# Windowed attention and routed experts: router columns copied on ScalarE, 64-row transposes, another order of stores and constants

## Chip, cores and metric

The kernel runs on one core of a Trainium2 chip. The metric is the device time of one execution in microseconds (us). The kernel before has three timed runs: 412.46, 412.88 and 413.97 us, median 412.88.

## What is computed

Attention over q, k, v of shape (8, 8, 576, 64) with a causal window of 64 positions, then a skip test, a router of 8 experts with one expert per token, and that expert's two-layer network:

```python
scores = (q @ k.transpose(0, 1, 3, 2)) / sqrt(64)
mask = (rel >= 0) & (rel < 64)               # rel = query position - key position
attn = softmax(where(mask, scores, -1e9))
x = (attn @ v).transpose(0, 2, 1, 3).reshape(4608, 512)
out = x.copy()
xc = x[x @ w_skip > 0]
probs = softmax(xc @ w_gate)                 # 8 experts
e_idx = argmax(xc @ w_gate)
y = probs[e_idx] * (relu(xc @ w1[e_idx]) @ w2[e_idx])
out[x @ w_skip > 0] = xc + y
```

## The kernel before

The 4608 tokens are cut into 36 tiles of 128 tokens, each of two blocks of 64 positions. Eight tiles of nine hold neighbouring blocks of one batch. The ninth (tiles 8, 17, 26 and 35) holds the last block of two batches.

The order of the work is written out by hand in a loop over `t` (lines 1182 to 1222), the "iterations" below. Every engine works through its own instructions in the order in which they are written there, and so do the queues from which transfers are issued (SP for nearly all loads and stores, POOL for the gathers and scatters). Iteration `t` writes, in this order:

- the loads that are due (`load_qk`, `load_v`, and their "tail" forms for the ninth tiles), issued from SP;
- `score(t + 1)` (lines 231 to 260): PE adds the mask band and writes q k^T for 8 heads into the two banks of `ps`, of which there are two copies; four quarters of PE's array, 64 by 64, work side by side;
- the gate products (`gate`, `gate_t`, lines 327 to 355): they work out v times the router's weights, 8 columns for experts and one for the skip test, which become columns 65 to 73 of each head in `vm`; column 64 is ones. Their results share the PSUM tag "t", two banks, with the transposes below;
- `lessen(t)` (lines 262 to 269): DVE takes the row maximum `mx` and subtracts it into `s`;
- `raise_e(t)` (line 273): ACT takes the exponential;
- `tile_out(t - 2)` with `av_tile` (lines 375 to 413): PE multiplies the transposed probabilities `ptm` with `vm` into `av`, of which there is one copy, two halves of 64 columns side by side; DVE then reads the sums of the probabilities in column 64 and forms `r`, their reciprocal (L395, L396), multiplies the 512 attention columns by it into `x` (L397), and the 72 router columns by it into `lh` (L403); `x` has four buffers;
- `transpose_p(t - 1)` (lines 275 to 283): PE transposes the probabilities of 8 heads, four at a time into one bank, and ACT copies each bank to `ptm`;
- `lower` and `tail_lower`: ACT copies that move the key block shared by two tiles.

Finished `x` tiles are stored to `out` by `store()` (lines 417 to 425), two tiles late (`SDELAY`), from SP. A tile of two batches is stored by one transfer (L425).

Routing works on groups of 8, 8, 6, 6 and 8 tiles. `lh` of a group holds 9 columns for 8 heads; `route` (line 505) adds up the heads, on GpSimd for the first four groups (`pool_part`, line 467) and on DVE for the last (`vector_part`, line 427). It then picks the expert and counts places; some of its steps are spread over several iterations by `yield`. After group 3 (tile 21) GpSimd works out `perm`, the order of the first two experts, for which SP waits before the first expert weights (L837). `load_constants` puts tables into `cf` and `vals` in iteration 3; `set_constants` makes small tables of them on GpSimd in iteration 5. `xgs` are nine buffers of 128x512, cleared in iteration 1; they later take gathered rows and, in between, pieces of the routing.

In the last two tiles, outside the loop, `transpose_p` writes into both banks of a `ps` tile (`into`). Then the expert stage runs to the end: weights are loaded in pieces of 512 KB (`raw`), split into a high and a low part, and multiplied with gathered rows.

Of the kernel before, what the change touches and what calls it, by code (L numbers as in the profile page):

```python
# [8 lines left out]
F32 = mybir.dt.float32  # L9
# [4 lines left out]
ALU = mybir.AluOpType  # L14
# [4 lines left out]
B, H, S, HD = 8, 8, 576, 64  # L19
N, D, E, F = 4608, 512, 8, 1024  # L20
P = 128
NB = S // 64
NT = N // P
# [19 lines left out]
NPOOL = 28  # L43
# [7 lines left out]
AHEADQ, AHEADV = 5, 4  # L51
SDELAY = 2
# [91 lines left out]
def window_attention_moe(ctx: ExitStack, tc, a, out):  # L144
    nc = tc.nc
# [6 lines left out]
    psum = ctx.enter_context(tc.tile_pool(name="psum", bufs=1, space=PSUM))  # L152
# [10 lines left out]
    ident = gid[:, 1]  # L163
# [22 lines left out]
    xp = rt.enter_context(tc.tile_pool(name="xp", bufs=2, side="right"))  # L186
    sm = rt.enter_context(tc.tile_pool(name="sm", bufs=3, side="right"))
# [83 lines left out]
    def raise_e(t):  # L271
        s = ss[t]
        nc.scalar.activation(s, s, AF.Exp, scale=0.125)  # L273

    def transpose_p(t, into=None):
        s = ss.pop(t)
        ptm = ptp.tile([P, 8, P], F32, name="ptm")
        for r in range(2):
            pt = into[:, r] if into is not None else psum.tile([P, 4, P], F32, name="pt", tag="t", bufs=2)
            for p in range(4):  # L280
                nc.tensor.transpose(pt[:, p], s[:, 4 * r + p], ident)  # L281
            nc.scalar.copy(ptm[:, 4 * r : 4 * r + 4], pt)  # L282
        pts[t] = ptm

    ss, pts, vs = {}, {}, {}
# [86 lines left out]
    def tail_lower(m, z):  # L372
        nc.scalar.copy(vms["t", m][0][:64, z], vms[4 * m + 2 * z + 1][64:, 3])

    def av_tile(t, lh, sums, av=None):
        blks = tiles[t]
        ptm, win = pts.pop(t), vs.pop(t)
        x = xp.tile([P, D], F32, name="x", bufs=XPB)
        if av is None:
            av = pav.tile([P, 2, 512], F32, name="av")  # L380
        banks["av"] = av
        for h in range(8):
            for hf in range(2):
                nc.tensor.matmul(  # L384
                    av[64 * hf : 64 * hf + 64, h // 4, (h % 4) * VW : (h % 4 + 1) * VW],
                    ptm[:, (h % 2) * 4 + h // 2, 64 * hf : 64 * hf + 64],
                    win[hf][:, h],
                    start=True,
                    stop=True,
                )  # L390
        if sums:
            sums()
        r = sm.tile([P, 2, 4], F32, name="r")
        src = av[:, :, : 4 * VW].rearrange("p z (h c) -> p z h c", c=VW)
        nc.vector.tensor_scalar(r, src[..., 64], 1e-9, None, op0=ALU.add)  # L395
        nc.vector.reciprocal(r, r)  # L396
        pace[0] = nc.vector.tensor_tensor(  # L397
            x.rearrange("p (z h c) -> p z h c", z=2, c=64),
            src[..., 0:64],
            r.unsqueeze(3).to_broadcast([P, 2, 4, 64]),  # L400
            op=ALU.mult,
        )
        nc.vector.tensor_tensor(  # L403
            lh.rearrange("p c (z h) -> p z h c", z=2),
            src[..., 65:74],
            r.unsqueeze(3).to_broadcast([P, 2, 4, 9]),
            op=ALU.mult,
        )
        if sums:
            sums()  # L410
        stores.append((x, blks))
        while len(stores) > (SDELAY if t < NT - 6 else 0):
            store()

    stores = []

    def store():
        x, ((b0, i0), (b1, i1)) = stores.pop(0)
        r0 = b0 * S + i0 * 64
        r1 = b1 * S + i1 * 64  # L420
        if r1 == r0 + 64:
            nc.sync.dma_start(out[r0 : r0 + P], x)
        else:
            both = out.rearrange("(b s) d -> b s d", s=S)[b0 : b1 + 1, i0 * 64 : i0 * 64 + 64]
            nc.sync.dma_start(both, x)  # L425

    def vector_part(t0, n, lh):
        lg = sm.tile([P, n, 9], F32, name="lg")
# [73 lines left out]
        yield "sums"  # L502
        return nd, ohb, gs

    def route(t0, n, lh):
        bn = lambda z: z.unsqueeze(1).to_broadcast([P, n, E])
        first_part = pool_part if t0 < NPOOL else vector_part
        nd, ohb, gs = yield from first_part(t0, n, lh)
        if t0 + n < NT:
            pr = banks["av"][:, 1, PRAT : PRAT + (n + 1) * E].rearrange("p (n e) -> p n e", e=E)  # L510
        else:
            pr = banks["late"].tile([P, n + 1, E], F32, name="pr", tag="g", bufs=1, padded_shape=[P, 64, E])
        nc.tensor.matmul(pr[:, 0:n], trib, ohb, start=True, stop=False, skip_group_check=True)
        for j in range(n):
            m = n - j
            nc.tensor.matmul(
                pr[:, j + 1 :],
                onesb,
                ohb[:, j : j + 1].to_broadcast([P, m, E]),
                start=False,  # L520
                stop=(j == n - 1),
                skip_group_check=True,
            )
        yield "added"
        ds = sm.tile([P, n, E], F32, name="gds")
        nc.vector.tensor_tensor(ds, pr[:, 0:n], bn(base), op=ALU.add)
        nc.vector.tensor_tensor(base, base, pr[:, n], op=ALU.add)
        nc.vector.reciprocal(ent[:, t0 : t0 + n, 1], gs)
        assert t0 < NCLOSE or "closed" in tables
        if t0 + n == NT:  # L530
            tables["counted"] = True
        here = rows[:, t0 : t0 + n]
        nc.gpsimd.tensor_tensor(ds, ds, ohb, op=ALU.mult)
        add_up(here, ds, E)
        nc.gpsimd.tensor_tensor(here, here, nd, op=ALU.add)
        later.append(enter(t0, n))
# [209 lines left out]
    xgs = [early.tile([P, D], F32, name=f"xg{i}") for i in range(NXG)]  # L746
# [8 lines left out]
    late = []  # L755
# [21 lines left out]
    def sums():  # L777
        step(late, held)
# [1 line left out]
    def listing():  # L780
        step(later, held2)

    grp = [0, 0, None]
    heads = [sum(GRP[:i]) for i in range(len(GRP))]

    def tile_out(t, av=None):
        if t in heads:
            n = GRP[heads.index(t)]
            grp[:] = [t, n, xp.tile([P, n, 9, H], F32, name="lh")]
        t0, n, lh = grp  # L790
        behind = None
        if held[0] == "sums" and held[1] >= WAIT.get(t0, 2):
            behind = sums
        elif held2[0] == "lists" and held2[1] >= LWAIT:
            behind = listing
        av_tile(t, lh[:, t - t0], behind, av)
        progress[0] = t + 1
        if t + 1 == t0 + n:
            late.append(route(t0, n, lh))

    progress = [0]

# [336 lines left out]
    first_of = [9 * (n // 4) + 2 * (n % 4) for n in range(NG)]  # L1139
    with tc.manual_schedule():  # L1140
# [16 lines left out]
        def when_at(t, f, n):  # L1157
            at.setdefault(max(t, 0), []).append((f, n))

        gate_at, lower_at, after_at = {}, {}, {}  # L1160
        for n in range(NG):
            if n >= 2:
                if n > 2:
                    when_at(first_of[n] - AHEADQ, load_qk, n)
                when_at(first_of[n] - AHEADV, load_v, n)
            gt = first_of[n] + 1 if n < 2 else first_of[n] - (2 if n > NSLOW else n == NSLOW)
            gate_at.setdefault(gt, []).append((gate_v, n))
            (after_at if n == 1 else gate_at).setdefault(gt + (n != 1), []).append((gate_vt, n))
            lower_at.setdefault(gt + 1, []).append((lower, n, 1))
            if n % 2:  # L1170
                lower_at.setdefault(gt + (1 if n == 3 else 2 * (n > 3)), []).append((lower, n, 0))
        for m in range(B // 2):
            z = 2 * (m == 0)
# [8 lines left out]
        for t in range(NT - 1):  # L1182
            m, r = divmod(t, 9)
            for f, n in at.get(t, ()):
                f(n)
            score(t + 1)
            gates = gate_at.get(t, ())
            if t == 0:
                keep_busy(5)
            for f, n in gates:  # L1190
                f(n)
            if t in (1, 2):
                transpose_p(t - 1)
            routes(1)
            if t != 3:
                lessen(t)
            raise_e(t)
            if t == 2:
                lessen(3)
            if BOTH <= t < NT - 2:  # L1200
                drip()
            if t >= 2:
                tile_out(t - 2)
            for f, n in after_at.get(t, ()):
                f(n)
            drip()
            routes(1)
            if t > 2:
                transpose_p(t - 1)
            if t == 1:  # L1210
                clear_rows()
            if t == 3:
                load_constants()
            if t == 5:
                set_constants()
            routes(1)
            for f, n, j in lower_at.get(t, ()):
                f(n, j)
            for _ in range(U0.count(t)):
                weight_dma_first()  # L1220
            if t == NT - 3:
                weight_hi(0)
# [197 lines left out]
    with tc.If(more > 0):  # L1420
        with tc.For_i(0, more, 1) as i:
# [15 lines left out]
            for qi in range(NQ):  # L1437
                both = []
                for w in range(2):
                    n = 2 * qi + w  # L1440
# [56 lines left out]
```

## Time and profile before

| | us |
|---|---|
| median of three runs | 412.88 |
| profiled execution | 411.98 |
| its span, first to last instruction | 410.2 |
| PE busy | 390.3 |
| DVE busy | 303.2 |
| ACT busy | 218.8 |
| GpSimd (POOL) busy | 154.2 |

Engines: PE is the matmul engine and PEld its weight loads, DVE the vector engine, ACT the scalar engine, POOL is GpSimd, SP issues transfers. "L397" is line 397 of the kernel. "x<-av,r" names what an instruction writes and reads. A busy engine is not necessarily a bottleneck: matmuls are pipelined, so that PE counts as busy over most of the span. The chain of work that ended last follows, from the last instruction back, what each step waited for. A share of the DMA engines is the mean over 16 engines. Attention runs from the start to about 163 us, experts from there to the end.

### The profile page before, as it was taken

What the parts mean: (1) busy time and instruction counts of PE and PEld (TensorE: products, weight loads), DVE (VectorE), ACT (ScalarE), POOL (GpSimd) and SP (SyncE); (2) the same over time, 40 slices, a digit from 0 to 9 for tenths busy, and PEclk for the clock granted to TensorE, in tenths of its full rate; (3) what the DMA queues carried; (4) which work ended last, traced back from release to release, by engine and by line L of the source; (5) the groups of instructions that cost most, each with busy time, mean ns of one, the idle gap of its engine ahead of it and who ended that gap; (6) DMA issues with size and microseconds to landing.
All of it is one profiled execution on the core that took longest, in us unless ns stands there. A gap on an engine that the chain in (4) does not pass through costs nothing.

```text
span 410.2 us, 11472 instructions
## 1 busy us (share of the span) xinstructions
PE 390.3 (95%) x4624; PEld 326.4 (80%) x4624; DVE 303.2 (74%) x537; ACT 218.8 (53%) x373; POOL 154.2 (38%) x276
## 2 busy tenths in 40 slices
PE   8998899999999979899999999999999999999794
PEld 4776687877787768788888988988888888988673
DVE  3786789899989896999558699475366476758871
ACT  2775876866876796445234453343254435533450
POOL 5121358166658678985305032041034030100110
PEclk9999999999999999999999999999999999999998
DMA  8999999998996885747506959554236786641510
GB/s 300 406 384 381 410 409 297 405 409 319 335 413 243 288 298 202 259 164 229 175 2 192 343 175 290 177 173 153 91 124 216 259 273 203 237 150 55 195 38 22
DMA packets 34480, 99.41 MB, mean 242 GB/s; under 512 B 4248, under 2 KB 5528, under 8 KB 34424
## 3 DMA queue, kind: packets, MB, share of 16 engines
q1 hardware_dynamic: 30360, 87.30, 60.1%
q0 software_dynamic: 3200, 9.58, 6.8%
q10 hardware_dynamic: 864, 1.77, 1.1%
q8 instruction: 37, 0.61, 0.6%
q14 instruction: 19, 0.16, 0.1%
HBM read 84.57 MB, written 14.39 MB: 241 GB/s over the span
## 4 chain that ended last, share of the span: by engine, by line
PE 49%; issue 18%; DMA 13%; DVE 10%; ACT 5%; POOL 2%; SPq 1%; POOLq 0%; DVEq 0%
PE av L384 6%; DMA out<-yo,les 5%; PE p L922 5%; PE p L923 4%; PE p L924 4%; PE pt L281 4%; PE ps L252 4%; DVE s L268 3%; DMA raw<-wq 2%; DMA gid<-gid 2%; DMA kt<-kT 2%; PE pw L331 2%; DVE mx L267 2%; PE yv L922 2%; PE yv L923 2%
## 5 line engine op out<-in xcount | busy, mean ns | idle before, releaser
L852 DVE TENSOR_TENSOR wlo<-raw,whi 128x1024 fp32r<-128x1024 f32 x69 | 85.4, 1245 | 15.8 <-ACT whi L848 15.5
L985 ACT ACTIVATE hh<-p 128x256 fp32r<-128x256 f32 (+4 forms) x56 | 22.9, 409 | 98.0 <-PE p L924 93.8
L848 ACT CAST whi<-raw 128x1024 fp32r<-128x1024 f32 x72 | 74.4, 1045 | 0.0
L1025 POOL DMA_INDIRECT out<-yo,les x18 | 17.6, 976 | 145.9 <-DVE yo L1016 136.1
L922 PE MATMUL p<-xp,whi 128*128 128x256 f32 (+4 forms) x192 | 58.2, 303 | 1.0 <-DVE hl L988 1.0
L988 DVE SCALAR_TENSOR_TENSOR hl<-p,hh 128x256 fp32r<-128x256 f32 (+4 forms) x56 | 25.1, 450 | 45.0 <-ACT hh L985 33.3
L923 PE MATMUL p<-xp,whi 128*128 128x256 f32 (+4 forms) x192 | 57.0, 297 | 0.0
L924 PE MATMUL p<-xp,wlo 128*128 128x256 f32 (+4 forms) x192 | 56.8, 296 | 0.0
L273 ACT ACTIVATE s<-s 128x1024 f32<-128x1024 f32 x36 | 38.1, 1058 | 29.5 <-DVE s L268 29.2
L267 DVE TENSOR_REDUCE mx<-ps 128x8 f32<-128x1024 f32 x36 | 43.6, 1210 | 5.9 <-PE ps L252 5.9
L268 DVE TENSOR_TENSOR s<-ps,mx 128x1024 f32<-128x1024 f32 x36 | 44.1, 1225 | 4.8 <-PE pt L281 0.3
L384 PEld LDWEIGHTS av<-vm,ptm 128*64 128x64 f32 x992 | 34.3, 136 | 11.0 <-issue 6.2
L384 PE MATMUL av<-vm,ptm 128*64 128x74 f32 x992 | 39.0, 230 | 2.2 <-DVE lh L403 1.3
L922 PEld LDWEIGHTS p<-xp,whi 128*128 128x128 f32 x192 | 36.2, 188 | 3.7 <-DVE hl L988 1.4
L281 PE MATMUL pt<-gid,s 128*128 128x128 f32 x272 | 37.2, 279 | 0.1
L923 PEld LDWEIGHTS p<-xp,whi 128*128 128x128 f32 x192 | 36.2, 188 | 0.7
L282 ACT COPY ptm<-pt 128x512 f32<-128x512 f32 x68 | 36.2, 580 | 1.1 <-PE pt L281 0.6
L924 PEld LDWEIGHTS p<-xp,wlo 128*128 128x128 f32 x192 | 36.2, 188 | 0.0
L252 PE MATMUL ps<-k,q 64*64 64x128 f32 x1024 | 33.5, 269 | 0.0
L252 PEld LDWEIGHTS ps<-k,q 64*64 64x64 f32 x1024 | 30.2, 133 | 2.0
L281 PEld LDWEIGHTS pt<-gid,s 128*128 128x128 f32 x272 | 29.2, 141 | 3.1 <-issue 0.4
L353 POOL COPY vm<-vm 64x1184 f32<-64x1184 f32 (+1 forms) x17 | 18.8, 1108 | 31.0 <-ACT vm L351 27.5
(240 smaller groups left out, 823.7 us busy)
## 6 DMA issues: line engine op xcount, KB each, us to landing
raw<-wq SPq DMA_DIRECT2D x72, 512.0 KB, 4.9
vm<-vp SPq DMA_DIRECT2D x16, 592.0 KB, 8.6
out<-x SPq DMA_DIRECT2D x36, 256.0 KB, 8.3
vT<-vT SPq DMA_DIRECT2D x16, 512.0 KB, 8.3
q<-qT SPq DMA_DIRECT2D x13, 512.0 KB, 9.5
k<-kT SPq DMA_DIRECT2D x8, 640.0 KB, 9.0
k<-kT SPq DMA_DIRECT2D x7, 512.0 KB, 8.8
kt<-kT SPq DMA_DIRECT2D x8, 256.0 KB, 9.5
```

Source lines behind the costliest of these rows:

```text
L252: nc.tensor.matmul(ps[64 * hf : 64 * hf + 64, r, p], q[h, p], k[h, :, p], start=False, stop=p == 3, skip_group_check=True,)
L267: nc.vector.tensor_reduce(mx, flat, axis=AX.X, op=ALU.max)
L268: pace[0] = nc.vector.tensor_tensor(s, flat, mx.unsqueeze(2).to_broadcast([P, 8, P]), op=ALU.subtract)
L273: nc.scalar.activation(s, s, AF.Exp, scale=0.125)
L281: nc.tensor.transpose(pt[:, p], s[:, 4 * r + p], ident)
L282: nc.scalar.copy(ptm[:, 4 * r : 4 * r + 4], pt)
L384: nc.tensor.matmul(av[64 * hf : 64 * hf + 64, h // 4, (h % 4) * VW : (h % 4 + 1) * VW], ptm[:, (h % 2) * 4 + h // 2, 64 * hf : 64 * hf + 6 ...
L848: nc.scalar.copy(ring[n % RING][0], raw_of[n])
L852: by.tensor_tensor(lo, raw_of[n], hi.bitcast(F32), op=ALU.subtract)
L922: nc.tensor.matmul(o, lh, rh, start=first, stop=False, skip_group_check=parts)
L923: nc.tensor.matmul(o, lh, rl, start=False, stop=False, skip_group_check=parts)
L924: nc.tensor.matmul(o, ll, rh, start=False, stop=last, skip_group_check=parts)
```

## The change

- `transpose_p` makes sixteen transposes of 64 rows in place of eight of 128, alternating between the two halves of the queries and their two banks. Both copies by ACT follow all sixteen; each now holds one half of the queries for all heads.
- In tiles 0 to 27 ACT copies the router columns unscaled, and GpSimd multiplies a whole group by `r` at the head of `route`. `r` of these tiles stands in two of the `xgs` buffers until then. Tiles 28 to 35 stay on DVE.
- Stores of tiles 0 to 7 are one tile late instead of two; a tile of two batches is stored by two transfers of 64 rows; q and k of group 4 are loaded one iteration later; constants are loaded in iteration 7 instead of 3 and set in 10 instead of 5.

```diff
     def transpose_p(t, into=None):
-        for r in range(2):
-            pt = into[:, r] if into is not None else psum.tile([P, 4, P], F32, name="pt", tag="t", bufs=2)
-            for p in range(4):
-                nc.tensor.transpose(pt[:, p], s[:, 4 * r + p], ident)
-            nc.scalar.copy(ptm[:, 4 * r : 4 * r + 4], pt)
+        both = [
+            psum.tile([P, 8, 64], F32, name="pt", tag="t", bufs=2)
+            if into is None
+            else into[:, r].rearrange("p a (b c) -> p (a b) c", c=64)
+            for r in range(2)
+        ]
+        halves = [slice(64 * hf, 64 * hf + 64) for hf in range(2)]
+        for h in range(8):
+            for pt, q in zip(both, halves):
+                nc.tensor.transpose(pt[:, h], s[q, h], ident[q, q])
+        for pt, q in zip(both, halves):
+            nc.scalar.copy(ptm[:, :, q], pt)
...
-    def av_tile(t, lh, sums, av=None):
+    def av_tile(t, lh, r, sums, av=None):
...
-        r = sm.tile([P, 2, 4], F32, name="r")
+        if t >= NPOOL:
+            r = sm.tile([P, 2, 4], F32, name="r")
...
-        nc.vector.tensor_tensor(
-            lh.rearrange("p c (z h) -> p z h c", z=2),
-            src[..., 65:74],
-            r.unsqueeze(3).to_broadcast([P, 2, 4, 9]),
-            op=ALU.mult,
-        )
+        cols = lh.rearrange("p c (z h) -> p z h c", z=2)
+        if t < NPOOL:
+            nc.scalar.copy(cols, src[..., 65:74])
+        else:
+            nc.vector.tensor_tensor(cols, src[..., 65:74], r.unsqueeze(3).to_broadcast([P, 2, 4, 9]), op=ALU.mult)
...
-        while len(stores) > (SDELAY if t < NT - 6 else 0):
+        while len(stores) > (1 if t < 8 else SDELAY if t < NT - 6 else 0):
             store()
...
-            both = out.rearrange("(b s) d -> b s d", s=S)[b0 : b1 + 1, i0 * 64 : i0 * 64 + 64]
-            nc.sync.dma_start(both, x)
+            nc.sync.dma_start(out[r0 : r0 + 64], x[:64])
+            nc.sync.dma_start(out[r1 : r1 + 64], x[64:])
...
-    def route(t0, n, lh):
+    def route(t0, n, lh, rs):
         first_part = pool_part if t0 < NPOOL else vector_part
+        if t0 < NPOOL:
+            by_head = rs.rearrange("p n z h -> p n (z h)").unsqueeze(2).to_broadcast([P, n, 9, H])
+            nc.gpsimd.tensor_tensor(lh, lh, by_head, op=ALU.mult)
...
+            rs = xgs[2 + heads.index(t) % 2][:, : n * H].rearrange("p (n z h) -> p n z h", z=2, h=4)
...
-                    when_at(first_of[n] - AHEADQ, load_qk, n)
+                    when_at(first_of[n] - AHEADQ + (n == 4), load_qk, n)
...
-            if t == 3:
+            if t == 7:
                 load_constants()
-            if t == 5:
+            if t == 10:
                 set_constants()
```

## Rows read from the trace of the kernel before

**Rows 1.** Page, part 1: busy us (share of the span) xinstructions.

```profile
PE 390.3 (95%) x4624; PEld 326.4 (80%) x4624; DVE 303.2 (74%) x537; ACT 218.8 (53%) x373; POOL 154.2 (38%) x276
```

**Rows 2.** Stretches: length, busy PE, PEld, DVE, ACT, POOL (instructions), PE clock, DMA share, GB/s.

```profile
42.00:60.00 18.00, 17.69 (x367) 14.19 (x368) 14.89 (x27) 13.61 (x26) 7.88 (x19) 1.00 1.03 409
...
42.00:125.00 83.00, 81.75 (x1697) 65.65 (x1699) 74.55 (x140) 61.72 (x110) 47.31 (x112) 1.00 0.99 375
42.00:150.00 108.00, 106.27 (x2200) 85.63 (x2201) 97.42 (x182) 81.34 (x144) 65.92 (x160) 1.00 0.93 347
```

**Rows 3.** Chain that ended last, 42 to 150 us: shares by line.

```profile
by line: PE av L384 21.1%; PE pt L281 14.8%; PE ps L252 12.4%; DVE s L268 9.1%; DVE mx L267 6.3%; PE pw L331 5.6%; PE ps L238 5.0%; DVE x L397 3.8%; issue 3.7%; PE pk L339 2.9%; ACT ptm L282 2.8%; ACT s L273 2.1%; DVE xg L600 1.8%; PE av L5
```

**Rows 4.** The same chain, pieces where PE paces: start us, us, what.

```profile
52.05 1.02 PE pt L281 x8
...
54.29 0.57 PE pw L331 x8
...
56.04 1.03 PE pt L281 x8
```

**Rows 5.** The same chain, pieces where DVE paces.

```profile
61.32 0.19 DVE lh L403
...
65.39 0.20 DVE lh L403
65.59 1.07 DVE xg L600
```

**Rows 6.** Timeline, DVE: start us, us, engine, line, operation, out<-in.

```profile
39.10 0.69 DVE L397 TENSOR_TENSOR x<-av,r 128x512 f32<-128x512 f32 x1
...
129.00 1.23 DVE L268 TENSOR_TENSOR s<-ps,mx 128x1024 f32<-128x1024 f32 x1
...
132.66 1.23 DVE L268 TENSOR_TENSOR s<-ps,mx 128x1024 f32<-128x1024 f32 x1
...
150.22 0.69 DVE L397 TENSOR_TENSOR x<-av,r 128x512 f32<-128x512 f32 x1
```

**Rows 7.** Timeline, PE; last row: durations of L281, ns min/median/max, first and last start.

```profile
107.89 1.25 PE L384 MATMUL av<-vm,ptm 128*64 128x74 f32 x32
...
109.08 1.09 PE L281 MATMUL pt<-gid,s 128*128 128x128 f32 x8
...
L281 PE MATMUL pt<-gid,s x272: 272/273/332, 11.7 to 150.2; 128*128 128x128 f32 x136
```

**Rows 8.** Timeline, SP's queue; last row: who waited for whom before 42 us.

```profile
26.19 0.33 SPq L176 DMA_DIRECT2D cf<-c_f  x1
...
28.36 0.33 SPq L210 DMA_DIRECT2D k<-kT  x1
...
29.85 0.35 SPq L422 DMA_DIRECT2D out<-x  x1
...
DVE x L397 <- DMA out<-x: 2.8, 1, 2.8
```

**Rows 9.** Groups of instructions by form, 60 to 160 us: busy us, mean ns.

```profile
L403 DVE TENSOR_TENSOR lh<-av,r 128x72 f32<-128x72 f32 x24 | 6.7, 281 | 0.0
...
L464 POOL TENSOR_TENSOR lh<-lh 128x288 f32<-128x288 f32 x1 | 0.8, 799 | 1.7 <-DVE lh L403 1.7
...
L368 ACT COPY vt<-pk 128x72 f32<-128x72 f32 x3 | 0.6, 210 | 0.0
```

**Rows 10.** Who waited for whom, 150 to 190 us: total, times, longest.

```profile
PE ps L281 <- ACT ptm L282: 2.2, 2, 1.5
```

**Rows 11.** SP's waits before 160 us; chain piece; page part 6, us to landing.

```profile
SPq L292 <- DMA out<-x: 7.7, 2, 4.1
...
165.84 5.93 DMA raw<-wq
...
raw<-wq SPq DMA_DIRECT2D x72, 512.0 KB, 4.9
```

More of the change, by code (lines that the diff above doesn't have):

```diff
@@ L781, in listing @@
         step(later, held2)
-    grp = [0, 0, None]
+    grp = [0, 0, None, None]
     heads = [sum(GRP[:i]) for i in range(len(GRP))]
@@ L788, in tile_out @@
             n = GRP[heads.index(t)]
-            grp[:] = [t, n, xp.tile([P, n, 9, H], F32, name="lh")]
-        t0, n, lh = grp
+            rs = xgs[2 + heads.index(t) % 2][:, : n * H].rearrange("p (n z h) -> p n z h", z=2, h=4)
+            grp[:] = [t, n, xp.tile([P, n, 9, H], F32, name="lh"), rs]
+        t0, n, lh, rs = grp
         behind = None
@@ L795, in tile_out @@
             behind = listing
-        av_tile(t, lh[:, t - t0], behind, av)
+        av_tile(t, lh[:, t - t0], rs[:, t - t0], behind, av)
         progress[0] = t + 1
         if t + 1 == t0 + n:
-            late.append(route(t0, n, lh))
+            late.append(route(t0, n, lh, rs))
     progress = [0]
```

## Prediction

> **What bounds the kernel now.** I read the profile from the outside in: busy shares, then the stretches, then the chain of work that ended last, then single instructions. The page gives PE 95%, DVE 74%, ACT 53% [rows 1], but a busy PE is pipelined time, so the shares alone decide nothing. The change lives in the attention stage, about 15 to 163 us of the 410.2 us span; the expert stage behind it is not touched and should only shift. In the table of stretches attention has PE at 106.3 and DVE at 97.4 of 108 us, ACT at 81.3, and the DMA engines are nearly full as well, 0.99 of their time up to 125 us [rows 2]. The reader should see three resources close together.
>
> The chain says who paces: from 42 to 150 us PE's attention lines hold 61.8% of it (av 21.1, pt 14.8, ps 12.4, pw 5.6, ps of the band 5.0, pk 2.9) and DVE most of the rest [rows 3]. Where PE paces, one tile is the time from one "pt" to the next, 56.04 - 52.05 = 3.99 us in a tile with a gate product of 0.57 [rows 4]. Where DVE paces, the chain goes through r, x, lh, mx, s, with lh worth 0.19 us (its duration is 0.28, but the next instruction starts before it ends) [rows 5, 9]. DVE undisturbed needs 132.66 - 129.00 = 3.66 us from one "s" to the next [rows 6]. The mean is longer: the x of tile 5 starts at 39.10 and that of tile 32 at 150.22, 27 intervals, 4.12 us each [rows 6]. The excess of 0.46 is where DVE waits for PE and where it does a group's routing, such as the 1.07 us of L600 [rows 5].
>
> **The change part by part.**
>
> Transposes. Eight 128-row transposes per tile become sixteen of 64 rows; each streams 64 columns of the identity, and the two halves lie on different rows of the array and in different banks. Eight take 1.09 us, the first 0.33 and the others 0.273, so they start (1.09 - 0.273 - 0.06) / 7 = 0.108 us apart [rows 7]. No 64-row transpose is in the trace. Nearest is av, also two halves of the array side by side: 32 matmuls of 74 columns, 0.23 each, in 1.25 us, so a pair every (1.25 - 0.23) / 15 = 0.068 us, and 64 columns by that rate 0.059. Weights of 128 columns load inside such a step: the first transpose is 332 - 273 = 59 ns longer than the rest, the time in which its weights came [rows 7]. Eight pairs then take 8 x 0.059 = 0.47 instead of 8 x 0.108 = 0.86, 0.39 us less PE per tile. Bounds: no overlap of the halves, 16 x 0.059 = 0.94 (+0.08); loads at the full 0.108 one after another, 1.73 (+0.87). I take 0.47, since av shows two halves side by side.
>
> The Trainium skill, "TensorE: Matmul & The Clock Gate", LDWEIGHTS (loading the stationary operand), says that a weight load costs its columns, whatever its rows: here 128 columns, 107 ns, for each half. By it the sixteen would need 0.86 us overlapped or 1.71 in sequence, and PE would gain nothing or lose; the 59 ns above disagree.
>
> Router columns. For tiles 0 to 27 DVE loses L403, 0.20 us per tile of its loop [rows 5]. ACT gains a copy of 128x72 out of PSUM; the like of it, L368, takes 0.21 us [rows 9]. It stands in ACT's order behind the exponential and ahead of the two copies of the transposed tile, so these, the gate copies and, through them, av wait for it. ACT has 26.7 us idle in 108 [rows 2] and mostly waits for s, so I take nothing for it here; the rival below has it on the path. The two copies also wait for all sixteen transposes rather than for four; in the steady tiles ACT is in its exponential then, which hides it.
>
> GpSimd gains one product per group of 6 or 8 tiles: 432 or 576 elements, from 0.80 us for 288 [rows 9] about 1.2 to 1.6 us, four times. GpSimd is idle 42 of 108 us [rows 2], and the routing behind it is spread over several tiles, so nothing is added; what it delays is that group's sums and perm, for which SP waits before the first expert weights.
>
> The middle, 27 intervals. DVE's own loop falls to 3.46. Least: only the 38% of the chain that is not PE's gains 0.20, 0.08 per tile, 2.2 us. Most: PE's whole 0.39 is followed, 10.5 us. I take 0.25, the 0.20 of the loop and a little of the excess that PE made: 27 x 0.25 = 6.75 us.
>
> The start. x of tile 4 waits 2.8 us for the store of tile 0 to leave its buffer [rows 8]. That store was issued at 29.85, behind cf (26.19), vals, and the k and q of group 4 (28.36) [rows 8]. The change puts it ahead of these: constants go to iteration 7, group 4's q and k one iteration later, stores of the first 8 tiles one earlier. It moves up by up to 3.7 us, so the wait can vanish. Late next are then q, k and v of group 4, pushed by two stores of 256 KB into full DMA engines. Bounds 0 and 2.8; I take 2.0. set_constants moves on the POOL queue to iteration 10, ahead of the first use of trib; it costs nothing as long as cf has landed. The row scales now stand in two gather buffers, cleared long before.
>
> The end. The last two tiles transpose into one tile of two banks, and there the second four waited for the copy of the first: 2.2 us of PE in two waits [rows 10]. All sixteen now come before any copy. Bounds 0 and 2.2; ACT is near its own limit there, so 1.3.
>
> Tail stores. Four stores across two batches become eight; one more issue of about 0.35 us each on SP, hidden by its waits. SP waited 7.7 us in two waits for such an out<-x before L292, and the chain has a raw load of 5.93 us, behind the last of these stores, against a median of 4.9 [rows 11]. I take 0, bounds 0 and 1.0.
>
> The Trainium skill, "DMA: Bandwidth & Descriptors", Why a DMA increments its semaphore by 16 and not by 1, says a transfer is spread over as many engines as divide the slowest dimension of both sides: two for a store shaped (2, 64, 512), sixteen for 64 rows. By that rule the 1.0 us would come in too; the waits agree, but no row here counts engines.
>
> Sum: 6.75 + 2.0 + 1.3 = 10.05 us. The profiled execution took 411.98 us (span 410.2), so 401.9; the median of the runs, 412.88, stands 0.90 above it, so **402.8 us**.
>
> **The rivals.**
> - PE gains nothing from the halves. Against it: av's pairs. For it: no transpose shows it. Then 2.2 + 2.0 + 1.3 = 5.5, 407.4 us.
> - Everything follows: 10.5 + 2.8 + 2.2 = 15.5, 397.4 us. Against it: ACT's added copy and full DMA engines.
> - The loads hold it. From 42 to 125 us 375 GB/s x 83 us = 31.1 MB moved; at the 409 GB/s of 42 to 60 us that is 76.1, so at most 6.9 us can be saved there, close to what I ask (20 of 27 tiles, 5.0, and the start). If half of that headroom can be had, 3.5, with 7 x 0.25 = 1.7 and 1.3: 6.5, 406.4 us [rows 2].
> - No change: ACT is in order, and s, exponential, columns, two copies, av, r is a loop. If it paces, DVE's 0.20 is exchanged for ACT's 0.21, the start is given back to late loads, and 1.3 stays: 411.6 us. For it: the chain passes through ACT already (ptm L282 2.8%, s L273 2.1%) [rows 3].
> - Slower: the halves' weights load at 0.108 us each in sequence. PE's tile grows by 0.87 to 4.86, and 4.7 where there is less gate work, against 4.12 now: 0.6 x 27 = 16.2, less 3.3 for start and end: 425.8 us. It decides above (0.86 + 0.13 + 0.12) / 16 = 0.07 us per half, when PE passes 4.12 and eats start and end. This is what the page's rule on loads would do in sequence. Against it: the 59 ns.
>
> **How the numbers follow.** Chances: forecast 0.50 (its own range 400 to 406), no PE gain 0.16, everything 0.08, loads 0.10, ACT loop 0.09, loads in sequence 0.07. All but the last two are faster by over 0.5%, about what a measurement of this kernel can tell: faster 0.84, same 0.09, slower 0.07. The range 398.5 to 409.5 leaves out both of these and about half of the case in which everything follows, 0.20 in all.
>
> **What would show it.** Sixteen transposes in 0.7 us or less, starts 0.03 apart (wrong at 1.1 or more); DVE's s to s 3.46 where undisturbed, and a mean interval of x near 3.87; no wait of L397 for out<-x near 35 us; the mid chain with less PE and more DVE and ACT; ACT's column copies at 0.21; no PE wait for ptm near 151 to 159 us; expert stage unchanged but earlier by 10 us. If ACT leads the chain, or DVE's idle time grows by what lh gave up, my middle term is wrong.

## The result, and the profile after

The changed kernel takes 416.86 us (median of 6 runs, 416.54 to 418.6) against 413.02 for the kernel before (412.28 to 414.07), a ratio of 1.0097, 95% interval 1.0079 to 1.0115. The forecast was 402.8 and the range ended at 409.5: slower, not faster. The profiled execution has a span of 414.7 us.

The page of the changed kernel, part 1, then two of its stretches (columns as in [rows 2]), then its chain from 42 to 150 us by line:

```profile
PE 384.5 (93%) x4912; PEld 320.0 (77%) x4912; DVE 301.1 (73%) x509; ACT 222.6 (54%) x401; POOL 158.8 (38%) x280
```

```profile
42.00:60.00 18.00, 15.29 (x350) 11.59 (x353) 12.47 (x21) 13.25 (x25) 8.05 (x16) 1.00 1.03 398
...
42.00:150.00 108.00, 96.72 (x2298) 76.21 (x2297) 90.72 (x151) 80.84 (x158) 67.57 (x160) 1.00 0.93 334
```

```profile
by line: PE av L391 17.6%; DVE x L405 7.1%; DVE s L268 6.8%; ACT ptm L289 6.7%; DVE mx L267 6.3%; ACT s L273 5.6%; issue 5.5%; PE pw L338 4.8%; DMA out<-x 4.6%; PE ps L252 3.7%; ACT lh L413 3.2%; PE pk L346 3.0%; DVE xg L610 3.0%; DVE xg L4
```

PE and DVE are both busy for less of the attention stage than in [rows 1, 2], and no engine took over: from 42 to 150 us PE falls from 106.3 to 96.7 and DVE from 97.4 to 90.7. The chain, which ran on PE for 62% [rows 3], is now in pieces: DVE's x, ACT's two ptm copies, ACT's exponential, and "issue", 5.5% against 3.7%. Work became shorter and waiting longer.

Where the time went is read off the starts of x. The timeline of the changed kernel has those of tiles 5 and 32 at 39.89 and 156.58 us, and around them two waits of ACT and PE (in brackets: idle time before the instruction, and what ended it).

```profile
31.35 0.71 PE L287 MATMUL pt<-gid,s 64*128 64x64 f32 x16
...
31.91 0.69 DVE L405 TENSOR_TENSOR x<-av,xg 128x512 f32<-128x512 f32 x1
...
32.69 0.29 ACT L413 COPY lh<-av 128x72 f32<-128x72 f32 x1 [0.99 <-DVE x L405]
32.80 1.08 ACT L289 COPY ptm<-pt 128x512 f32<-128x512 f32 x2
33.45 0.16 PEld L338 LDWEIGHTS pw<-vT,gid 128*32 128x32 f32 x8 [0.42 <-ACT ptm L289]
...
39.89 0.69 DVE L405 TENSOR_TENSOR x<-av,xg 128x512 f32<-128x512 f32 x1
...
40.22 1.04 PE L252 MATMUL ps<-k,q 64*64 64x128 f32 x28
43.01 0.43 PE L252 MATMUL ps<-k,q 64*64 64x128 f32 x4 [1.76 <-issue]
...
156.58 0.69 DVE L405 TENSOR_TENSOR x<-av,r 128x512 f32<-128x512 f32 x1
```

Before, tiles 5 and 32 stood at 39.10 and 150.22 [rows 6], and tile 35 at 162.50; here tile 35 stands at 166.56. So the span's 4.5 us are: 0.8 up to tile 5; 116.69 - 111.12 = 5.6 more in the 27 intervals of the middle (4.32 each against 4.12, where 3.87 was forecast); 9.98 - 12.28 = 2.3 less in the last three tiles; and 0.4 more behind. The start gave nothing, the middle went the wrong way, the end gave more than forecast.

Two waits stand out, and each comes from a part of the change. At 32.69 ACT's column copy has waited 0.99 us for VectorE's x, and ACT's ptm copies, which are ready, stand behind it in order; so do the gate product and av. At 43.01 PE has stood still for 1.76 us behind the 28th of a tile's 32 score matmuls, with "issue" as the cause: it waited for nothing that the profile shows. The line of the column copy, and who waited from 42 to 150 us (total, times, longest; "xg" in L403 is `r`, which stands in an `xgs` buffer in these tiles):

```profile
L413 ACT COPY lh<-av x28: 287/291/294, 19.1 to 137.3; 128x72 f32<-128x72 f32 x28
...
  DVE x L405: 13.9, 18
```

```profile
ACT lh L413 <- DVE x L405: 8.6, 12, 1.4
DVE xg L403 <- PE av L391: 7.0, 8, 2.4
PEld pk L346 <- ACT ptm L289: 6.6, 13, 0.8
PEld pw L338 <- ACT ptm L289: 5.7, 12, 0.8
```

The copy waits 13.9 us for x in 18 of 28 tiles. It is in the program: the copy waits for a semaphore of VectorE, since both engines read the av banks. The Trainium skill, "PSUM — Partial Sum Buffer", PSUM bank collisions raise a hardware error, says that two engines must not access one bank in the same 32 partitions at a time, reads against reads included, and that the compiler adds a dependency for it. The waits agree; what happens without the dependency no run here shows.

### The profile page after: what moved, and what is told of

Same layout as the page of the kernel before. It is cut to its first block, busy times and chain, and to the rows that moved or that the text cites. A ratio compares the mean times of both kernels' runs of the same rounds, so it can differ in the third digit from the quotient of the medians.

```text
span 414.7 us, 12103 instructions
## 1 busy us (share of the span) xinstructions
PE 384.5 (93%) x4912; PEld 320.0 (77%) x4912; DVE 301.1 (73%) x509; ACT 222.6 (54%) x401; POOL 158.8 (38%) x280
## 3 DMA queue, kind: packets, MB, share of 16 engines
q10 hardware_dynamic: 864, 1.77, 1.1%
## 4 chain that ended last, share of the span: by engine, by line
PE 48%; issue 14%; DVE 9%; DMA 7%; POOL 5%; ACT 5%; POOLq 0%; DVEq 0%; ACTq 0%
PE p L933 6%; PE av L391 5%; PE p L934 5%; PE p L935 5%; DMA out<-yo,les 5%; PE yv L933 3%; PE yv L934 3%; PE yv L935 3%; PE yw L933 2%; DVE x L405 2%; PE yw L934 2%; PE yw L935 2%; DVE s L268 2%; ACT ptm L289 2%; POOL wlo L863 2%
## 5 line engine op out<-in xcount | busy, mean ns | idle before, releaser
L391 PEld LDWEIGHTS av<-vm,ptm 128*64 128x64 f32 x992 | 36.0, 136 | 13.0 <-issue 7.0
L391 PE MATMUL av<-vm,ptm 128*64 128x74 f32 x992 | 41.6, 231 | 3.5 <-issue 2.4
L252 PE MATMUL ps<-k,q 64*64 64x128 f32 x1024 | 34.5, 269 | 2.6 <-issue 2.6
L287 PE MATMUL pt<-gid,s 64*128 64x64 f32 x544 | 24.9, 229 | 1.9 <-ACT vm L358 1.1
L933 PE MATMUL yv<-whi,hh 128*128 128x512 f32 x64 | 25.9, 405 | 0.0
```

What stands on the lines that cost most here:

```text
L252: nc.tensor.matmul(ps[64 * hf : 64 * hf + 64, r, p], q[h, p], k[h, :, p], start=False, stop=p == 3, skip_group_check=True,)
L391: nc.tensor.matmul(av[64 * hf : 64 * hf + 64, h // 4, (h % 4) * VW : (h % 4 + 1) * VW], ptm[:, (h % 2) * 4 + h // 2, 64 * hf : 64 * hf + 6 ...
L933: nc.tensor.matmul(o, lh, rh, start=first, stop=False, skip_group_check=parts)
```

## The experiments

Theories as they stand in the expectations: 1, the column copy waits for x and holds ACT's queue; 2, the halves fill both banks at once and their copies come later; 3, the later loads and moved stores cost; 4, formed after the first four kernels: the halves double PE's transposing instructions, and those come late.

**One part at a time.** Four kernels: the change with the columns back on VectorE; before with the halves alone; before with the columns alone; before with the moved stores, constants, load of group 4 and split tail stores alone.

```
cols_on_dve, against the change (r is again a tile of its own for every t)
-        if t < NPOOL:
-            nc.scalar.copy(cols, src[..., 65:74])
-        else:
-            nc.vector.tensor_tensor(cols, src[..., 65:74], r.unsqueeze(3).to_broadcast([P, 2, 4, 9]), op=ALU.mult)
+        nc.vector.tensor_tensor(cols, src[..., 65:74], r.unsqueeze(3).to_broadcast([P, 2, 4, 9]), op=ALU.mult)
...
-            nc.gpsimd.tensor_tensor(lh, lh, by_head, op=ALU.mult)
halves_only, against before: the change's hunk of transpose_p
cols_only, against before: its hunks of av_tile (but for the stores), route and tile_out
order_only, against before
-        while len(stores) > (SDELAY if t < NT - 6 else 0):
+        while len(stores) > (1 if t < 8 else SDELAY if t < NT - 6 else 0):
...
-            nc.sync.dma_start(both, x)
+            nc.sync.dma_start(out[r0 : r0 + 64], x[:64])
+            nc.sync.dma_start(out[r1 : r1 + 64], x[64:])
...
-                    when_at(first_of[n] - AHEADQ, load_qk, n)
+                    when_at(first_of[n] - AHEADQ + (n == 4), load_qk, n)
...
-            if t == 3:
+            if t == 7:
                 load_constants()
-            if t == 5:
+            if t == 10:
                 set_constants()
```

> The changed kernel with one part undone: the router columns stay on DVE, scaled there, with no product on GpSimd. Theory 1 (ScalarE's column copy waits for x on DVE and holds up the copies behind it): most of the loss goes, 403 to 409 us, and ScalarE has no wait for DVE x. Theory 2 (the half transposes take both banks at once and delay their copies): no help, 415 to 418 us. Theory 3 (the later load of group 4 and the moved stores): 413 to 416 us, with PE waiting inside a score near 41 us.

> The kernel before with the 64-row transposes alone. Theory 1: nothing is in their way, 0.4 us of PE per tile where PE paces, 406 to 410 us. Theory 2: slower than before, 414 to 417 us. Theory 3: as theory 1.

> The kernel before with the router columns alone (copy on ScalarE, product on GpSimd). Theory 1: slower than before by 4 to 9 us, 417 to 422 us, the mean interval of x above 4.25 us, ScalarE idle ahead of the column copy until DVE x. Theories 2 and 3: no loss here, 410 to 413 us.

> The kernel before with the stores, the constants and the load of group 4 in the other order, and the tail stores in two parts. Theory 1 and 2: 409 to 412 us, since the wait for out<-x near 35 us goes. Theory 3: 414 to 417 us, with PE waiting inside the score of group 4.

Measured: cols_on_dve 415.37 us, 1.0044 of before (1.0019 to 1.0070); halves_only 416.73, 1.0079 (1.0051 to 1.0108); cols_only 416.48, 1.0079 (1.0055 to 1.0102); order_only 410.98, 0.9949 (0.9928 to 0.9971). The order is the only part that gains, and theory 3 falls. Columns and halves each cost 3 to 4 us by themselves, and with the columns taken out of the change the time is far above the 403 to 409 us of theory 1. In halves_only the sixteen transposes are fast and ACT has no column copy, yet PE stands still again. Its timeline (PE) and its stretches of 2 us:

```profile
42.36 0.44 PE L252 MATMUL ps<-k,q 64*64 64x128 f32 x4 [1.77 <-issue]
...
43.69 2.24 PE L391 MATMUL av<-vm,ptm 128*64 128x74 f32 x32
...
79.04 0.73 PE L391 MATMUL av<-vm,ptm 128*64 128x74 f32 x15 [1.06 <-issue]
...
91.26 0.33 PE L346 MATMUL pk<-gid,vw 128*128 128x128 f32 x1 [1.22 <-issue]
```

```profile
44.00:46.00 2.00, 2.00 (x34) 1.85 (x32) 0.02 (x1) 1.76 (x3) 0.00 (x0) 0.50 1.04 422
```

The gaps cut groups of one operation in two (av after 17 of 32, pk after one of two), where no semaphore is waited for. Behind the 1.77 us the granted clock is 0.50, the lower of the two levels, and av takes 2.24 us where it took 1.25 [rows 7]. This traced execution took 418.87 us, 2.1 above the median of its kernel; another 3.4 us at the lower clock, near 163 us, are in it too.

Counting PE's instructions, loads and matmuls, from the first in the trace, these gaps stand behind numbers 705, 961, 1217, 1473, 3009, 3521 and so on: 193 + 256 k, every one. PE's instructions come by DMA, in packets of 16 KB on a queue of their own (the page has 39 such packets here, 37 before, for about 9,900 and 9,400 instructions: 256 each). The queues of halves_only in three stretches, 39 to 39.9, 39.9 to 41 and 42 to 43 us:

```profile
q1 hardware_dynamic: 93, 0.37, 101.4%
...
q1 hardware_dynamic: 174, 0.42, 98.3%
q8 instruction: 1, 0.02, 5.4%
...
q1 hardware_dynamic: 161, 0.40, 101.0%
```

The packet starts at 39.97, with the DMA engines full, and PE goes on at 42.36, 2.4 us later; at each gap of 0.3 us or more it is 2.3 to 2.7 us. Before, a packet starts 2.2 us behind a block boundary on the mean; with 2.4 us until it is of use that leaves time, since a block of 256 instructions lasts 6.3 us: from 16 to 150 us no boundary is late. With the halves the packet starts 3.4 us behind the boundary and a block lasts 6.0: 10 of 23 boundaries are late by over 0.3 us, 9.0 us in all. The whole change has 3 such, 3.3 us in all; that the waiting for columns slows PE down and so gives the packets time is the likely reason. It fits cols_on_dve, which takes the columns out of the change and gives back only some 1.5 us: 11 of its boundaries are late, 9.3 us in all.

**The columns in another place; the halves where the DMA engines are not full; and the halves with fewer loads.**

```
cols_after, against cols_only (columns() issues what stands in behind_ptm)
-            nc.scalar.copy(cols, src[..., 65:74])
+            behind_ptm.append(lambda: nc.scalar.copy(cols, src[..., 65:74]))
...
         if t + 1 == t0 + n:
+            columns()
             late.append(route(t0, n, lh, rs))
...
                 transpose_p(t - 1)
+            columns()
halves_late, against before: transpose_p
+        if t >= 28:
+            (the change's hunk)
+        else:
             (as before)
before_light, against before; halves_light, against halves_only
-        if parts[0][0] == 0:
+        if n >= 6:
+            qs[n] = qs[5]
+        elif parts[0][0] == 0:
...
-            other.dma_start(q[:, s:e], a["qT"][b, :, 4 * g + s : 4 * g + e])
+            if n < 6:
+                other.dma_start(q[:, s:e], a["qT"][b, :, 4 * g + s : 4 * g + e])
...
+        if n < 6:
+            kept["vT"] = vtp.tile([P, 4, 256], F32, name="vT")
+            nc.sync.dma_start(kept["vT"], a["vT"][b, g])
+        vTs[n] = kept["vT"]
```

> Before with the router columns on ScalarE and GpSimd, and the copy put behind the two copies of the transposed tile of the same iteration (for the last tile of a group it stays where it was). Theory 1 (the copy waits for VectorE's x of its tile, and holds the two ptm copies, the gates and through them av): no ptm copy waits for x any more, the mean interval of x from tile 5 to 32 falls to before's 4.12 or under it (4.0), and the time is 409 to 413. Rival (what costs is not the place but the work itself: GpSimd's product late, the routing's reads of the av bank waiting for ScalarE, or the copy's 0.29 us on ScalarE): it stays at 415 to 417.

> Before with the 64-row transposes only from tile 28 on. Theory 4 (the halves double the instructions of the transposes; PE's instructions come in packets of 16 KB, one for 256 instructions, each asked for when the block before is used up; where the DMA engines are full the packet comes late and PE stands still in mid-group; where they are not full it comes in time): from tile 28 on the DMA engines are no longer full, so there is no gap in mid-group, PE gains its 0.4 us per tile where it paces, and the two waits for ptm at 152 and 158 us go: 410 to 413, before or up to 2.5 under it. Rival, theory 2 (the halves need both banks at once and their copies start later, everywhere): 7 of 28 tiles at +0.14 us, 413.5 to 414.5.

> Before without the loads of q and vT from group 6 on (their tiles of group 5 are read again): about 1 MB of 3.1 MB less per group from tile 13 on, which leaves those data wrong and the instruction streams of PE, VectorE and ScalarE as they were. It is the base for halves_light. Every theory: if the loads pace nothing, within 2 us of before (411 to 413); if they do pace, shorter by up to 4. The start of the 16 KB packets behind a block boundary of PE, 2.1 us on the mean now, falls under 1 us after about 70 us.

> The same left out, with the 64-row transposes. Theory 4: after about 70 us the instruction packets start at once, so no gap of over 0.3 us in mid-group is left there (six stood in halves_only between 70 and 130 us), and the mean interval of x from tile 16 to 32 is below that of before_light by 0.1 to 0.3 us; with the early gaps of halves_only still there (about 2 us) the time is 0 to 3 us under before_light. Rival, theory 2: the halves still cost about 0.14 us per tile, so the interval is above that of before_light and the time 3 to 4 us over it.

cols_after: 414.6 us, 1.0030 (1.0006 to 1.0054). Behind the ptm copies the columns cost 1 us instead of 3.5; so the place was most of the loss, but the gain expected of VectorE's shorter loop didn't come, and 414.6 lies above what theory 1 gave. halves_late: 410.87 us, 0.9911 (0.9878 to 0.9945), as theory 4 has it, though with one gap of 1.09 us at 142 us, again at 193 + 256 k. The waits for ptm in the last two tiles [rows 10] are gone, and x of tile 35 starts 1.5 us earlier than before.

In the pair with fewer loads only the attention stage is to be compared (the other values of q and vT send the tokens elsewhere, and the expert stage is long). The stretch of 60 to 130 us and the starts of x in tiles 16 and 32, before_light first, then halves_light:

```profile
60.00:130.00 70.00, 68.57 (x1423) 54.91 (x1422) 64.51 (x121) 50.64 (x90) 43.59 (x109) 1.00 0.70 228
...
84.91 0.69 DVE L401 TENSOR_TENSOR x<-av,r 128x512 f32<-128x512 f32 x1
150.19 0.69 DVE L401 TENSOR_TENSOR x<-av,r 128x512 f32<-128x512 f32 x1
```

```profile
60.00:130.00 70.00, 64.91 (x1585) 52.09 (x1581) 65.18 (x122) 50.52 (x90) 44.35 (x111) 1.00 0.71 232
...
85.35 0.69 DVE L408 TENSOR_TENSOR x<-av,r 128x512 f32<-128x512 f32 x1
149.87 0.69 DVE L408 TENSOR_TENSOR x<-av,r 128x512 f32<-128x512 f32 x1
```

With the DMA share at 0.71 (halves_only has 0.95 in this stretch), halves_light has no gap over 0.3 us at a boundary from 56 to 145 us, where halves_only has six: the halves' loss is the late packets, and theory 2 falls. But 64.52 against 65.28 us for 16 intervals is a gain of 0.05 us per tile. PE's busy time fell by 3.7 us of 70 and the tile hardly shortened: even undisturbed, the halves are worth next to nothing in the middle. And before_light answers the rival of the prediction in which the loads hold the middle: with the share at 0.70 instead of 0.97, x of tile 32 starts at 150.19, where it started at 150.22 [rows 6].

**Does the gap follow the block, or the work?** 64 PE instructions more ahead of everything:

```
halves_shift, against halves_only
         keep_busy(12)
+        few = pav.tile([P, 2, 512], F32, name="av")
+        for _ in range(32):
+            nc.tensor.matmul(few[:, 0, 0:2], onesb, onesb[:, 0:2], start=True, stop=True, skip_group_check=True)
```

> Halves_only with 32 matmuls of two columns added behind the twelve that keep PE busy at the start, 64 more PE instructions (32 loads, 32 matmuls) ahead of everything. Theory 4: in halves_only every gap in mid-group stands at instruction 193 + 256 k of PE, loads and matmuls counted from the first; here the gaps stand at the same places of that count, so 64 instructions earlier in the work (after the 28th ps matmul of a tile no longer; the one at 42.36 us is found about 1 us earlier in another group). The sum of gaps stays at 5 to 10 us, the time at 414 to 418. Rival (the gaps belong to a place in the work: a bank, a late load, a semaphore): they stay behind the same matmuls as in halves_only, 64 later in the count.

```profile
57.24 0.88 PE L252 MATMUL ps<-k,q 64*64 64x128 f32 x21 [0.36 <-issue]
63.53 0.68 PE L391 MATMUL av<-vm,ptm 128*64 128x74 f32 x15 [0.84 <-issue]
...
122.13 0.45 PE L252 MATMUL ps<-k,q 64*64 64x128 f32 x8 [1.14 <-issue]
```

The six gaps in mid-group stand behind 2241, 2497, 3521, 4545, 4801 and 5057, 193 + 256 k once more, that is 64 instructions earlier in the work. One other pause, in av of the tail tile near 50 us, has 1866 in halves_only and 1930 here: it kept its place in the work and is no part of this. The sizes were missed: 7 late boundaries and 4.5 us of gaps where 5 to 10 us were expected, and 412.88 us (one run, before beside it 413.79) where 414 to 418 were. Where the boundaries fall in the tile matters for how many are late.

**The two relieved together, and what can be kept.**

```
both_light: halves_light with the edits of cols_only and cols_after
after_moved, against the change: the edit of cols_after
best_28 and best_34, against order_only: transpose_p
+        if t >= 28:          (best_34: if t >= NT - 2:)
+            (the change's hunk)
+        else:
             (as before)
```

> As halves_light (no loads of q and vT from group 6 on, which leaves their data wrong), with the router columns moved as in cols_after too. Its total is not to be compared, only the attention stage. If the step for the middle was right but for the late packets and the place of the copy (both VectorE's loop and PE's shorter), the mean interval of x from tile 16 to 32 is 3.8 to 3.9, against 4.08 in before_light and 4.03 in halves_light. Rival (a third loop, s to exponential to transposes to ptm to av to x, or the routing's work on VectorE, holds the tile): 4.0 or more.

> The whole change, with ScalarE's column copy put behind the two copies of the transposed tile. Theory 1 and 4 together: the copy's place was worth 2 us alone (cols_only 416.5, cols_after 414.6); but without it PE runs faster through its instructions and meets more late packets (9 us of gaps in halves_only, 4 in the whole change): 413.5 to 416, that is 1 to 3 us gained of the 4 lost. Rival (the two copies from both banks cost by themselves): 416 to 418.

> Order_only with the 64-row transposes in the last two tiles alone, those that transpose into one tile of two banks. If the waits for ptm at 152 and 158 us are worth what halves_late showed there (the intervals before x of tiles 33 and 35 shorter by 1.5 and 1.2 us) and add to order_only's 2.0: 408 to 409, 1.0 to 1.2 per cent under before. Rival (what is gained at the end is lost to the loads of the first expert weights): 410.5 to 411.5, order_only again.

> The same with the 64-row transposes from tile 28 on. Theory 4: 16 KB packets late by chance at one or two block boundaries between 130 and 150 us, where the DMA engines are about 0.7 busy; halves_late lost 1.1 us at one and gained 0.4 before: 408 to 410.5, no better than best_34. Rival (the halves save PE time wherever the DMA engines are not full): 406 to 408.

both_light shortens PE's work and VectorE's with few late packets left, and tiles 16 to 32 take 64.28 us, 4.02 each: the rival's value. The timeline shows the loop that holds a tile in which VectorE has no routing to do; first both_light, then a tile of before:

```profile
126.73 1.23 DVE L271 TENSOR_TENSOR s<-ps,mx 128x1024 f32<-128x1024 f32 x1
...
127.99 1.06 ACT L276 ACTIVATE s<-s 128x1024 f32<-128x1024 f32 x1 [2.26 <-DVE s L271]
...
128.30 0.69 DVE L409 TENSOR_TENSOR x<-av,xg 128x512 f32<-128x512 f32 x1
...
128.95 1.05 ACT L292 COPY ptm<-pt 128x512 f32<-128x512 f32 x2
...
129.89 0.30 ACT L417 COPY lh<-av 128x72 f32<-128x72 f32 x1
130.25 1.23 DVE L271 TENSOR_TENSOR s<-ps,mx 128x1024 f32<-128x1024 f32 x1
...
130.34 1.26 PE L395 MATMUL av<-vm,ptm 128*64 128x74 f32 x32
...
131.63 0.17 DVE L407 TENSOR_SCALAR xg<-av 128x8 f32<-128x8 f32 x1 [0.15 <-PE av L395]
...
132.07 0.69 DVE L409 TENSOR_TENSOR x<-av,xg 128x512 f32<-128x512 f32 x1
```

```profile
71.59 1.23 DVE L268 TENSOR_TENSOR s<-ps,mx 128x1024 f32<-128x1024 f32 x1
...
72.84 1.06 ACT L273 ACTIVATE s<-s 128x1024 f32<-128x1024 f32 x1
...
73.76 0.28 DVE L403 TENSOR_TENSOR lh<-av,r 128x72 f32<-128x72 f32 x1
...
73.81 1.05 ACT L282 COPY ptm<-pt 128x512 f32<-128x512 f32 x2
73.90 1.21 DVE L267 TENSOR_REDUCE mx<-ps 128x8 f32<-128x1024 f32 x1
...
75.11 1.25 PE L384 MATMUL av<-vm,ptm 128*64 128x74 f32 x32
75.25 1.23 DVE L268 TENSOR_TENSOR s<-ps,mx 128x1024 f32<-128x1024 f32 x1
...
76.42 0.17 DVE L395 TENSOR_SCALAR r<-av 128x8 f32<-128x8 f32 x1
```

From the end of s: exponential, two ptm copies, av, then r. Before this takes 76.42 - 72.82 = 3.60 us (av is done at 3.54, and r does not wait for it), and VectorE's own way from the end of one s to the end of the next 76.48 - 72.82 = 3.66: the two are nearly equal. In both_light VectorE's way is 131.48 - 127.96 = 3.52, but the loop through ACT, with the column copy in it, is 131.63 - 127.96 = 3.67, and r waits for av. In such a tile a shorter VectorE buys nothing: from x of tile 26 to x of tile 27 both_light takes 132.07 - 128.30 = 3.77 us, before_light 3.67:

```profile
126.64 0.69 DVE L401 TENSOR_TENSOR x<-av,r 128x512 f32<-128x512 f32 x1
...
130.31 0.69 DVE L401 TENSOR_TENSOR x<-av,r 128x512 f32<-128x512 f32 x1
```

In a tile in which the routing gives VectorE more to do, the shorter loop does count (tile 23 to 24: 4.00 us in before_light, 3.87 in both_light). The mean of 4.02 is made of both kinds, and of waits for av: 2.2 us from 86 to 150 us, most of them put down to the routing's matmuls into av.

after_moved: 416.43 us, 1.0049 (1.0023 to 1.0074), just above the expected band; by the ratios half of the change's loss of 1.0097 is gone. As expected, PE without the wait for x meets more late packets: 8 boundaries and 9.2 us of them from 16 to 150 us.

best_34: 409.72 us, 0.9897 (0.9875 to 0.9920); best_28: 409.37, 0.9905 (0.9881 to 0.9929). Both beat the kernel before by 1% and order_only by half of that; best_34 just missed its 408 to 409. They can't be told apart: best_28 gains at tile 29 and has a gap of 0.79 us at 140 us.

## Why the prediction was wrong

**Transposes: the size right, its worth wrong.** Sixteen take 0.71 us against 1.09, 0.38 less, where the text had 0.39; the rival in which PE's transposes gain nothing, and the one in which their loads come in sequence, are out. The rule of the Trainium skill, "TensorE: Matmul & The Clock Gate", LDWEIGHTS, cited there, gives an estimate of 0.86 us or more; the trace has 0.71 with its sixteen loads, and the measurement decides. The 59 ns against it were misread, though: they are not the time of a load. One load takes 141 ns in L281 of before and 139 in L287 of the change, and the sixteen overlap. What the step left out, without a term, is the count of instructions: 4912 matmuls against 4624, each with a load, and the stream has to be brought in through DMA engines that [rows 2] shows full. The Trainium skill, "Runtime: NRT & Kernel Launch", Instruction fetch mechanics, names blocks of 256 instructions, the next fetched while the current one runs, and calls the cost of a boundary mostly hidden. The block size agrees with the count above; the hiding held before and fails with the halves, by up to 1.8 us at a boundary.

**Router columns: the step that failed first.** The text set ACT's copy at 0.21 us and "nothing" on the path. It takes 0.29 (the like of it that was read, 0.21, is the tail tile's), and the length is the smaller error: it waits for x, 13.9 us in 18 of 28 tiles, with the copies of the transposed tile behind it. The cover named for ACT's idle time, waiting for s, lies at another point of the tile. GpSimd's product was about right: 1.1 us for 432 elements.

**The middle: 0.25 us per tile was the term that was wrong by the most.** It took 0.20 from VectorE's loop as if that loop were alone. Even alone it was not worth that: the lines of before above have L403 at 73.76 and VectorE's next instruction at 73.90, 0.14 us later, and so it is in 26 of the 27 tiles from 5 to 31; the 0.19 and 0.20 were pieces of a chain. Tiles 28 to 31 keep L403, so 23 x 0.14 = 3.2 us was there where 27 x 0.20 = 5.4 was counted. Nor was there much that PE could give. The chain has 62% on PE, but VectorE works beside it; who VectorE waited for from 42 to 128 us, before:

```profile
DVE r L395 <- PE av L384: 2.2, 3, 1.0
DVE r L395 <- PE av L556: 1.5, 2, 0.8
DVE r L395 <- PE av L516: 0.6, 2, 0.4
```

That is 4.3 us in 86, so most of the 10.5 us of the upper bound could not be had from PE. The loop through ACT, s to exponential to ptm to av to r, was written down only in the rival for no change (0.09), with VectorE's 0.20 exchanged for ACT's 0.21. That rival had the mechanism of the tiles without routing; its 411.6 us lacks the wait for x and the late packets. The measurement to make was there in the trace of before: 3.60 beside 3.66. With the wait for x and the late packets taken away, both_light against before_light, the tile falls from 4.08 to 4.02 us: 27 x 0.06 = 1.6 us in place of 6.75.

**The start: right, and lost.** order_only has the forecast 2.0 us: x of tile 4 starts at 32.60 and doesn't wait for a store. In the whole change columns and halves had used it up by tile 5, which starts at 39.89 (36.74 in order_only). Here the two parts meet: the transposes need both banks of the "t" buffer before the first copy, so near 22 us fifteen of sixteen wait for the vm copy. With the halves alone that is 0.17 us; in the whole change it is 1.15, since the vm copy stands in ACT's queue behind a column copy that has waited 1.26 us for x.

**The end: right in kind, 1.3 forecast, 2.3 (whole change, last three tiles) to 2.6 (halves_late) measured.** The two ptm waits of 2.2 us went whole.

**Tail stores: 0, right.** SP's wait for out<-x ahead of L292 [rows 11] is gone in order_only, with no share of its own that these runs could tell from the rest of the order.

**What stays open.** Why a packet starts 3.4 us behind its boundary with the halves and 2.2 without; and what cols_after's last 1 us is. Its trace has the loss early: tiles 5 to 16 take 47.40 us against 46.08 before, tiles 16 to 32 take 65.17 against 65.04. The longer ACT loop, which is there in both stretches, is at most a part of it; no run tested that.

## What to carry to other kernels

Before an engine's work is shortened, close the loops, not the engines: from one s to the next through every engine in turn, and see whether a second loop is as long. What an instruction is worth to a loop is the time to the start of the next one on its engine, read in several tiles. Work that is moved to an idle engine stands in that engine's queue, so ask what it waits for there and who is behind it. A cheaper operation in twice as many instructions is not free where the DMA engines are full: count the instructions against the time in which the next 256 must arrive.

## What the runs showed of the hardware

A block of 256 PE instructions is of use 2.2 to 2.7 us after its packet starts, at the late boundaries of all these kernels; with the DMA engines at 0.95 to 0.97 of their time from 60 to 130 us, the packet started 2.2 us (before) to 3.4 us (halves_only) behind the boundary on the mean. Such a gap has no cause in the profile but "issue", and shows by cutting a group of equal matmuls in two. After the gap of 1.77 us in halves_only the granted clock was 0.50 from 44 to 46 us, and av cost 1 us more; after one of 1.76 in the whole change no such fall is in its row (1.00 from 42 to 60). With 64 PE instructions without use put ahead of all others, the gaps came to 4.5 us where halves_only had 9.0.
